# One transfer for V, a masked four-pass softmax and 128-column products in a decode step

## The chip, the cores and the metric

The kernel runs on one core of one Trainium2 chip. The metric is the device time of one execution in microseconds (us). Beside the unprofiled times there is one profiled execution; its span runs from the first to the last instruction, and the time of the execution is a little longer than its span. Engines are named as the profile names them: PE is TensorE's matrix multiplication and PEld its loading of weights, DVE is VectorE, ACT is ScalarE, POOL is GpSimd, SP is SyncE, which issues nearly all transfers of this kernel.

## The reference

One token of 1024 numbers passes two branches side by side, and their sum with the input is the result. All inputs and the output are bf16. `_layernorm` subtracts the mean and divides by the standard deviation.

```python
xn = layernorm(x)                                # [1, 1, 1024]
# branch A: 32 query heads over 4 key/value heads, the last W = 4096 of 65536 cached positions
q = (xn @ wq).reshape(32 heads, 128)             # wq [1024, 4096]
k = k_cache[:, :, Sk - W:, :]                    # [4 heads, 4096, 128], each for 8 query heads
v = v_cache[:, :, Sk - W:, :]
p = softmax(q @ k.T * 128 ** -0.5)
a = (p @ v).reshape(4096) @ wo                   # wo [4096, 1024]
# branch B
y = layernorm(xn)
b = gelu(y @ w1 + b1) @ w2 + b2                  # w1 [1024, 3584], w2 [3584, 1024]
out = x + a + b
```

With one token every weight is used once. wq and wo are 8 MB each, w1 and w2 7 MB each, the parts of K and V that are read 4 MB each: the 39.86 MB that the profile has as read from HBM.

## The kernel before

**What lies where.** `BIG` has 60 pieces of 1024 columns on each of 128 partitions. At first, pieces 0 to 31 hold wq (`WA`) and pieces 32 to 59 hold w1 (`W1`). Later W2 (28 pieces) lies in wq's place, and wo, 32 pieces, behind it. `KV` holds K as loaded, and later V; `KT` holds the turned K, and its end is used for the turned probabilities `PT`.

**The order of the transfers.** SP's queue is an order written out by hand: wq in two parts, K in two parts (two heads each), w1, then V in two parts, W2 in two parts (16 and 12 pieces) and wo in four (16, 11, 4 and 1 pieces). The first five are issued at once. A V part (L312) waits until VectorE has turned the K part in whose place it goes. W2 (issued by the helper `load_chunks`, L159; wo has L319) waits until the eight groups of q matmuls are done (`done["q"]`), since it overwrites wq. wo waits until the seven groups of the hidden layer are done (`done["h"]`), since it overwrites w1. ACT issues three small transfers (x, b1, b2).

**The order on TensorE.** A product that spreads x over the partitions; 38 matmuls on zeros as a warm-up, which begin when POOL has prepared all constants (`C["consts"]`); 64 matmuls for q, as soon as wq has landed; 32 for the scores, each half of K as soon as VectorE has turned it (L284); 56 for the hidden layer (`done["h"]`); a small product that adds up the sums of the exponentials and puts the sum where it is needed (`done["tot"]`, L484); four small ones that turn the hidden layer (`done["hT"]`); 32 for P times V (L496, `done["pv"]`); then eleven rounds of eight matmuls: seven for W2 and four for the first 16 pieces of wo. A round starts when `s_feed` has reached its count; POOL adds to that semaphore as W2's parts land and when the attention's result is ready (L407 to L414), and wo's first transfer adds to it too. The last 16 pieces of wo are multiplied in small matmuls of 32 columns as their transfers land, ending in L510.

**Softmax and P times V.** The scores lie in four banks of PSUM (`S`), 2048 columns on 128 partitions. VectorE finds the maximum of each row (L333), joins the partitions' maxima (L337, L339) and writes the bias `NMB` (L342). ScalarE then takes the exponential of all 2048 columns in one instruction with the sum of each row (L345), and VectorE turns the result in blocks of 32 (L349). A matmul of P times V takes 128 columns of weights from `PT`, in steps of 64, so that two neighbours overlap by half, and 2 x 256 columns of V:

```python
C["exp"] = ACT.mark(act.activation(
    out=Pb[:, :], in_=S, func=ACTF.Exp, bias=NMB[:, 0:1], scale=SCALE, accum_out=SUMP[:, 0:1]))
last = add(bank(1), PT[:, bass.ds(i * 256 + u * 64, 128)], V3[:, :, bass.ds(i * 1024 + u * 256, 256)])
```

VectorE reads rows 0 to 63 of the product and takes the right columns of each query head by the mask `HALF` while it divides by the sum (L380), adds them up (L385), turns the result (L388, L391), and ScalarE writes it as weights for wo (L394, L395).

Of the kernel before, what the change touches and what calls it, by code (L numbers as in the profile page):

```python
# [5 lines left out]
ALU = mybir.AluOpType  # L6
ACTF = mybir.ActivationFunctionType
AX = mybir.AxisListType

D = 1024  # L10
# [3 lines left out]
DH = 128  # L14
REP = HQ // HKV
SK = 65536
W = 4096
FC = F // 128
# [4 lines left out]
W2_CHUNKS = [16, 12]  # L23
# [4 lines left out]
PAIRS = 2  # L28
FAR = -1e30
XP = 72  # L30
TAIL = 16
# [4 lines left out]
ROUND = 4  # L36
# [17 lines left out]
def bass_parallel_sum__sliding_block_cached__mixer_channel_mlp__decode_kernel(  # L54
# [13 lines left out]
    SCALE = float(DH) ** -0.5  # L68
# [13 lines left out]
    s_w2 = sems("s_w2", len(W2_CHUNKS))  # L82

    DVE = Track(nc, "S_DVE")
    ACT = Track(nc, "S_ACT")
    POOL = Track(nc, "S_POOL")
    done = {n: nc.alloc_semaphore(f"S_PE_{n}") for n in (
        "x", "h", "hT", "q", "sc", "pv", "tot", "fin")}
    s_feed = nc.alloc_semaphore("S_FEED")

    def sb(name, shape, d):
        return nc.alloc_sbuf_tensor(name, shape, d)

    f32, bf16 = dt.float32, dt.bfloat16
    identb = sb("identb", [128, 128], bf16)
    identf = sb("identf", [128, 128], f32)
    onesb = sb("onesb", [2, 128], bf16)
    FLIP = sb("FLIP", [8, 8], bf16)
    E4 = sb("E4", [32, 4 * 128], bf16)
    B64 = sb("B64", [128, 64], f32)  # L100
    HALF4 = sb("HALF4", [64, 4], f32)
    HALF = sb("HALF", [64, PAIRS], f32)
    OTHER = sb("OTHER", [2, 128], bf16)
    ALT = sb("ALT", [2, 512], bf16)
    EDGE = sb("EDGE", [2, 132], bf16)
# [13 lines left out]
    MX2 = sb("MX2", [128, 2], f32)  # L119
    MX8 = sb("MX8", [32, 8], f32)  # L120
    MXR = sb("MXR", [32, 1], f32)
    NMB = sb("NMB", [128, 1], f32)
    Pb = sb("Pb", [128, 2048], bf16)
    XN = Pb[:, 0:1024]
    XM = Pb[:, 1024:2048]
    Q32 = Pb[:, 0:512]
    QTB = Pb[:, 512:1024]
    SUMP = sb("SUMP", [128, 1], f32)
    REC = sb("REC", [64, 1], f32)
    ON = sb("ON", [32, DH], f32)  # L130
    ONT = sb("ONT", [32, DH], f32)
    O2 = sb("O2", [128, 32], f32)
# [2 lines left out]
    ONM = QBD[0:32, :].bitcast(f32)  # L135
    KV = sb("KV", [128, 16384], bf16)
    KT = sb("KT", [128, 16384], bf16)
    PT = KT[:, 16384 - 2112:16384]
    BIG = sb("BIG", [128, KC * NQ + KC * F], bf16)
    WA, W1 = BIG[:, 0:KC * NQ], BIG[:, KC * NQ:KC * NQ + KC * F]  # L140
    W2 = WA[:, 0:FC * D]
    PS = nc.alloc_psum_tensor("PS", [128, 8 * 512], f32)
    PSb = PS[:, :].bitcast(bf16)

    def bank(n, rows=128, first=0):
        return PS[first:first + rows, n * 512:(n + 1) * 512]
# [23 lines left out]
    def pool_wait():  # L170
        pool.wait_ge(POOL.sem, POOL.cnt)
# [11 lines left out]
    POOL.mark(pool.memset(identf[:, :], 0.0))  # L183
    POOL.mark(pool.memset(FLIP[:, :], 0.0))
    POOL.mark(pool.memset(EDGE[:, :], 0.0))
    POOL.mark(pool.memset(HALF4[:, :], 1.0))
    POOL.mark(pool.memset(OTHER[:, :], FAR))
    POOL.mark(pool.memset(ALT[:, :], 0.0))
    POOL.mark(pool.memset(E4[:, :], 0.0))
# [15 lines left out]
    POOL.mark(pool.affine_select(  # L205
        out=ALT[:, :].rearrange("p (x g) -> p x g", g=2), in_=ALT[:, :].rearrange("p (x g) -> p x g", g=2),
        pattern=[[0, 256], [-1, 2]], compare_op=ALU.not_equal, fill=1.0, base=0, channel_multiplier=1))
    POOL.mark(pool.affine_select(
        out=HALF4[:, :], in_=HALF4[:, :], pattern=[[-16, 4]], compare_op=ALU.is_ge, fill=0.0,
        base=0, channel_multiplier=1))  # L210
    pool_wait()
    POOL.mark(pool.affine_select(
        out=HALF4[:, :], in_=HALF4[:, :], pattern=[[16, 4]], compare_op=ALU.is_ge, fill=0.0,
        base=15, channel_multiplier=-1))
    POOL.mark(pool.memset(GO[:, :], 0.0))
    pool_wait()
    POOL.mark(pool.tensor_tensor(out=HALF[:, :], in0=HALF4[:, 0:2], in1=HALF4[:, 2:4], op=ALU.add))  # L217
    C["consts"] = POOL.cnt

    act.wait_ge(POOL.sem, C["QBD"])  # L220
# [5 lines left out]
    def pairs(cache, c):  # L226
        return cache[0, 2 * c:2 * c + 2, SK - W:SK, :].rearrange("g (m i) d -> m g (i d)", m=64)
# [9 lines left out]
    def dve_wait():  # L237
        dve.wait_ge(DVE.sem, DVE.cnt)

    def layernorm_stats(src, n, name):  # L240
# [34 lines left out]
        XZ[:, :].rearrange("p (r w) -> p r w", r=KC)[:, :, 7:104:32], XNT[:, :].unsqueeze(2).to_broadcast([128, KC, 4])))  # L275
    dve.wait_ge(POOL.sem, C["consts"])
    DVE.mark(dve.tensor_reduce(
        out=B64[:, :].rearrange("p (k r) -> p k r", k=2),
        in_=identf[:, :].rearrange("p (q r) -> p r q", q=4).unsqueeze(1).to_broadcast([128, 2, 32, 4]),
        axis=AX.X, op=ALU.add))  # L280

    def turn_k(n):
# [23 lines left out]
    for n in range(2, 4):  # L306
        turn_k(n)

    V = KV[:, :]
    for c in range(PAIRS):  # L310
        sp.wait_ge(DVE.sem, C["kt", 2 * c + 1])
        sp.dma_start(V[:, c * 8192:(c + 1) * 8192], pairs(A_v_cache, c)).then_inc(s_v, 16)  # L312
    sp.wait_ge(done["q"], 8)
    load_chunks(W2, w2_p, W2_CHUNKS, D, s_w2)
    sp.wait_ge(done["h"], 7)
    c0 = 0
    for j, n in enumerate(WO_CHUNKS):
        first = (FC + c0) * D
        sp.dma_start(BIG[:, first:first + n * D], wo_flat[:, c0 * D:(c0 + n) * D]).then_inc(s_wo[j] if j else s_feed, HALF_FEED)  # L319
        c0 += n  # L320

# [16 lines left out]
    dve_wait()  # L338
    DVE.mark(dve.tensor_reduce(out=MXR[:, :], in_=MX8[:, :], axis=AX.X, op=ALU.max))  # L339
    dve_wait()  # L340
    for b in range(4):
        C["nmb"] = DVE.mark(dve.tensor_scalar(  # L342
            out=NMB[32 * b:32 * b + 32, :], in0=MXR[:, :], scalar1=-SCALE, scalar2=None, op0=ALU.mult))
    act.wait_ge(DVE.sem, C["nmb"])
    C["exp"] = ACT.mark(act.activation(  # L345
        out=Pb[:, :], in_=S, func=ACTF.Exp, bias=NMB[:, 0:1], scale=SCALE, accum_out=SUMP[:, 0:1]))

    dve.wait_ge(ACT.sem, C["exp"])
    C["d_pt"] = DVE.mark(dve.transpose(PT[:, 0:2048], Pb[:, :]))  # L349
    act.wait_ge(done["h"], 7)  # L350
    C["a_h8"] = ACT.mark(act.activation(out=H8, in_=bank(0, 8), func=ACTF.Copy))

# [19 lines left out]
        out=spread(0, FC // ROUND), in0=rows_of(HT[:, :]), in1=rows_of(U2[:, :]), op=ALU.mult))  # L372

    dve.wait_ge(done["tot"], 1)
    DVE.mark(dve.reciprocal(out=REC[:, :], in_=PS[0:64, 3 * 512:3 * 512 + 1]))
    dve_wait()
    dve.wait_ge(done["pv"], 8)
    for i in range(2):
        rows = slice(32 * i, 32 * i + 32)
        DVE.mark(dve.scalar_tensor_tensor(  # L380
            out=ONM.rearrange("p (i c d) -> p i c d", i=2, c=PAIRS)[:, i],
            in0=PS[rows, 512:1024].rearrange("p (c i d) -> p i c d", c=PAIRS, i=2)[:, i], scalar=REC[rows, 0:1],
            in1=HALF[rows, :].unsqueeze(2).to_broadcast([32, PAIRS, DH]), op0=ALU.mult, op1=ALU.mult))
    dve_wait()
    DVE.mark(dve.tensor_reduce(  # L385
        out=ON[:, :], in_=ONM.rearrange("p (g d) -> p d g", g=4), axis=AX.X, op=ALU.add))
    dve_wait()
    DVE.mark(dve.transpose(ONT[:, :], ON[:, :]))  # L388
    dve_wait()
# [33 lines left out]
    def add(to, lhsT, rhs, **place):  # L423
        return pe.matmul(to, lhsT=lhsT, rhs=rhs, start=False, stop=False, skip_group_check=True, **place)  # L424
# [56 lines left out]
        last.then_inc(done["h"], 1)  # L481

    pe.wait_ge(ACT.sem, C["exp"])
    pe.matmul(PS[0:64, 3 * 512:3 * 512 + 1], lhsT=B64[:, :], rhs=SUMP[:, :]).then_inc(done["tot"], 1)  # L484
    pe.wait_ge(ACT.sem, C["a_h8"])
    for c in range(4):
        last = add(turned[:, c], H8[:, c:512:4], FLIP[:, 0:7])
        if c == 0:
            pe.wait_ge(s_v, 32)
    last.then_inc(done["hT"], 1)  # L490

    pe.wait_ge(DVE.sem, C["d_pt"])
    V3 = V.rearrange("p (c x) -> p c x", c=PAIRS)
    with pe.Fori(0, 8) as i:
        for u in range(4):
            last = add(bank(1), PT[:, bass.ds(i * 256 + u * 64, 128)], V3[:, :, bass.ds(i * 1024 + u * 256, 256)])  # L496
        last.then_inc(done["pv"], 1)

    pe.wait_ge(DVE.sem, C["d_GT"])
    with pe.Fori(0, ROUNDS) as t:  # L500
        pe.wait_ge(s_feed, turn)
        pe.reg_add(turn, turn, 2 * HALF_FEED)
        for u in range(ROUND):
            for a in range(2):
                add(bank(7), GO[:, bass.ds(t * STEP + (LEAD + 2 * u - ROW - a), 128)],
                    BIG[:, bass.ds(t * (ROUND * D) + (u * D + a * 512), 512)])

    c0 = TAIL
    def add_held(to, lhsT, rhs, column):
# [5 lines left out]
    for j, n in enumerate(WO_ROWS[WO_HEAD:]):  # L515
        held = c0 + n == 32
        if held:
            for a in range(4):
                first = LEAD + 2 * (c0 - TAIL) - (0 if a % 2 else ROW)
                pe.ldweights(OT[:, first:first + 32], tile_position=(0, 32 * a))  # L520
        pe.wait_ge(s_wo[WO_HEAD + j], 16)
        for c in range(c0, c0 + n):
            rhs = BIG[:, (FC + c) * D:(FC + c + 1) * D]
            for a in range(4):
                first, column = LEAD + 2 * (c - TAIL) - (0 if a % 2 else ROW), 7 * 512 + a // 2 * 256
                to, of = PS[32 * a:32 * a + 32, column:column + 256], rhs[:, TAIL_AT[a]:TAIL_AT[a] + 256]
                if held:
                    last = add_held(to, OT[:, first:first + 32], of, 32 * a)
                else:
                    last = add(to, OT[:, first:first + 32], of, tile_position=(0, 32 * a))  # L530
        c0 += n
# [31 lines left out]
```

## Time and profile before

| | |
|---|---|
| median of 3 runs | 98.81 us (98.64 to 98.84) |
| time of the profiled execution | 98.62 us |
| its span | 97.2 us |
| granted TensorE clock | 1.00 |
| PE busy | 79.4 us (82%) |
| DVE busy | 39.0 us (40%) |
| ACT busy | 11.2 us (12%) |
| read from HBM | 39.86 MB, 410 GB/s over the span |

The profile's page divides the span into 40 equal slices and gives each engine's busy share in tenths; the row DMA gives the mean busy share of the core's 16 DMA engines. Its chain that ended last is followed back from the last instruction, each step to what released it. A group of instructions is given with its line, engine, operation, out<-in tiles, count, busy time, mean, and the idle time before it with what ended that. DMA issues are given with their size and the time from issue to landing; since all of SP's transfers pass one queue, that time holds the wait behind earlier transfers too. Matmuls that come from a helper all have its line (L424), so they are told apart by their tiles: `BIG,XZ` is q, `KT,QBD` the scores, `BIG,YZ` the hidden layer, `KV,KT` P times V, `BIG,GO` W2 and wo.

### The profile page before, as it was taken

How to read it: one execution, taken by the hardware profiler on the slowest of the kernel's cores; microseconds unless marked ns; L12 is line 12 of the kernel's file. 1: busy time of each engine (PE TensorE's matmuls, PEld its weight loads, DVE VectorE, ACT ScalarE, POOL GpSimd, SP SyncE). 2: the span in 40 equal slices, each digit the busy share in tenths (PEclk: the TensorE clock that was granted, in tenths of full speed). 3: DMA queues.
4: the chain of work that ended last, by engine and by line, in shares of the span. 5: the costliest groups of instructions: out<-in, count | busy, mean ns of one | idle time of the engine just before them, and what ended most of it. 6: DMA issues, size and time to landing. Idle time of an engine off the chain costs nothing.

```text
span 97.2 us, 1412 instructions
## 1 busy us (share of the span) xinstructions
PE 79.4 (82%) x389; PEld 33.4 (34%) x400; DVE 39.0 (40%) x54; ACT 11.2 (12%) x20; POOL 9.9 (10%) x27
## 2 busy tenths in 40 slices
PE   0000899977999999999299999899999999979982
PEld 0000134423444432343134444333334344334451
DVE  0000589840079986999945450060029000000001
ACT  0870000060000006000003500200000100000001
POOL 6999400000000000000000000000000000000000
DMA  2998888899999988889999999999899999899990
GB/s 64 651 473 378 378 378 378 378 458 432 401 431 549 590 378 378 378 378 401 415 431 431 431 492 431 431 458 394 384 475 499 458 431 431 368 389 436 388 379 3
DMA packets 1989, 39.88 MB, mean 410 GB/s; under 512 B 322, under 2 KB 324, under 8 KB 452
## 3 DMA queue, kind: packets, MB, share of 16 engines
q1 hardware_dynamic: 1876, 39.85, 95.7%
q10 hardware_dynamic: 112, 0.01, 0.1%
q8 instruction: 1, 0.02, 0.1%
HBM read 39.86 MB, written 0.00 MB: 410 GB/s over the span
## 4 chain that ended last, share of the span: by engine, by line
DMA 54%; PE 30%; DVE 11%; issue 1%; SPq 1%; ACT 1%
DMA BIG<-in_A_wo_dram 32%; PE PS L424 30%; DMA BIG<-in_A_wq_dram 22%; DVE KT L284 9%; SPq L319 1%; DVE Pb L292 1%; DVE QBD L303 1%; ACT Pb L290 1%; DVE Pb L401 0%; SPq L159 0%; PE PS L510 0%
## 5 line engine op out<-in xcount | busy, mean ns | idle before, releaser
L424 PE MATMUL PS<-BIG,GO 128*128 (+1 forms) x137 | 21.5, 334 | 1.8 <-POOLq L414 0.8
L284 DVE STREAM_TRANSPOSE KT<-KV 128x4096 bf16<-128x4096 bf16 x4 | 17.5, 4424 | 6.9 <-DMA KV<-in_A_k_cache_dram 6.9
L424 PE MATMUL PS<-BIG,XZ 128*128 x64 | 14.0, 379 | 1.3 <-DMA BIG<-in_A_wq_dram 1.3
L424 PEld LDWEIGHTS PS<-BIG,GO 128*128 (+1 forms) x148 | 9.9, 97 | 13.5 <-issue 5.9
L424 PE MATMUL PS<-BIG,YZ 128*128 x56 | 12.4, 380 | 0.1
L428 PE MATMUL PS<-QBD 128*128 128x512 bf16 x38 | 10.1, 434 | 0.4 <-POOL HALF L217 0.4
L424 PEld LDWEIGHTS PS<-BIG,XZ 128*128 x64 | 6.2, 97 | 9.0 <-issue 2.7
L424 PE MATMUL PS<-KT,QBD 128*128 x32 | 7.4, 380 | 1.9 <-DVE KT L284 1.9
L420 PE MATMUL PS<-XBRP,onesb 1*128 1x512 bf16 x2 | 1.0, 617 | 9.7 <-DMA XBRP<-in_A_x_dram 9.7
L424 PE MATMUL PS<-KV,KT 128*128 x32 | 8.3, 381 | 0.5
L401 DVE CAST Pb<-PS 64x256 bf16<-64x256 f32 x1 | 0.4, 416 | 20.0 <-PE PS L510 20.0
L424 PEld LDWEIGHTS PS<-BIG,YZ 128*128 x56 | 5.4, 96 | 7.1 <-issue 1.2
L428 PEld LDWEIGHTS PS<-QBD 128*128 128x128 bf16 x38 | 4.0, 108 | 6.9 <-issue 3.7
L242 DVE BATCH_NORM_STATS2 BN<-PS 128x6 f32<-128x512 f32 x2 | 1.3, 688 | 10.7 <-PE PS L420 10.7
L424 PEld LDWEIGHTS PS<-KT,QBD 128*128 x32 | 3.0, 97 | 6.2 <-issue 3.3
L424 PEld LDWEIGHTS PS<-KV,KT 128*128 x32 | 3.1, 96 | 5.3 <-issue 3.8
L380 DVE SCALAR_TENSOR_TENSOR QBD<-PS,REC,HALF 32x256 f32<-32x256 f32 x2 | 0.9, 474 | 6.8 <-PE PS L424 6.8
L345 ACT ACTIVATE Pb<-PS,NMB 128x2048 bf16<-128x2048 f32 x1 | 2.0, 1967 | 13.8 <-DVE NMB L342 13.8
L420 PEld LDWEIGHTS PS<-XBRP,onesb 1*128 1x128 bf16 x2 | 0.1, 108 | 9.7 <-DMA XBRP<-in_A_x_dram 9.7
L349 DVE STREAM_TRANSPOSE KT<-Pb 128x2048 bf16<-128x2048 bf16 x1 | 2.3, 2310 | 2.1 <-ACT Pb L345 2.1
L333 DVE TENSOR_REDUCE MX<-PS 128x1 f32<-128x1024 f32 x2 | 2.4, 1206 | 1.3 <-PE PS L424 1.3
L354 DVE COPY HT<-PS 128x28 f32<-128x28 f32 x1 | 0.2, 207 | 6.2 <-PE PS L424 6.2
(81 smaller groups left out, 42.1 us busy)
## 6 DMA issues: line engine op xcount, KB each, us to landing
BIG<-in_A_wq_dram SPq DMA_DIRECT2D x1, 7168.0 KB, 21.1
BIG<-in_B_w_dram SPq DMA_DIRECT2D x1, 7168.0 KB, 46.0
KV<-in_A_k_cache_dram SPq DMA_DIRECT2D x2, 2048.0 KB, 27.7
KV<-in_A_v_cache_dram SPq DMA_DIRECT2D x2, 2048.0 KB, 14.5
BIG<-in_B_w_dram SPq DMA_DIRECT2D x1, 4096.0 KB, 20.5
BIG<-in_A_wo_dram SPq DMA_DIRECT2D x1, 4096.0 KB, 23.1
BIG<-in_B_w_dram SPq DMA_DIRECT2D x1, 3072.0 KB, 27.1
BIG<-in_A_wo_dram SPq DMA_DIRECT2D x1, 2816.0 KB, 29.4
```

Of the source, the lines that this page charges most:

```text
L242: DVE.mark(dve.bn_stats(out=BN[:, 12 * n + 6 * i:12 * n + 6 * i + 6], in_=src[:, 512 * i:512 * i + 512]))
L284: C["kt", n] = DVE.mark(dve.transpose(KT[:, n * 4096:(n + 1) * 4096], KV[:, n * 4096:(n + 1) * 4096]))
L290: C["q32"] = ACT.mark(act.activation(out=Q32, in_=bank(7), func=ACTF.Copy))
L292: C["qtb"] = DVE.mark(dve.transpose(QTB, Q32))
L303: C["d_QBD"] = DVE.mark(dve.tensor_copy(to, of))
L319: sp.dma_start(BIG[:, first:first + n * D], wo_flat[:, c0 * D:(c0 + n) * D]).then_inc(s_wo[j] if j else s_feed, HALF_FEED)
L333: C["mx"] = DVE.mark(dve.tensor_reduce(out=MX2[:, n:n + 1], in_=S[:, 1024 * n:1024 * n + 1024], axis=AX.X, op=ALU.max))
L345: C["exp"] = ACT.mark(act.activation(out=Pb[:, :], in_=S, func=ACTF.Exp, bias=NMB[:, 0:1], scale=SCALE, accum_out=SUMP[:, 0:1]))
L349: C["d_pt"] = DVE.mark(dve.transpose(PT[:, 0:2048], Pb[:, :]))
L420: last = pe.matmul(bank(2 + i), lhsT=onesb[0:1, :], rhs=XB[0:1, 8 * i:8 * i + 8, :])
L424: return pe.matmul(to, lhsT=lhsT, rhs=rhs, start=False, stop=False, skip_group_check=True, **place)
L428: pe.matmul(to, lhsT=zeros[:, 0:128], rhs=zeros[:, 0:512], skip_group_check=True, **how)
```

## The change

V no longer goes into K's place in two transfers of two heads, but into the first 16 pieces of `BIG` (wq's place) in one transfer of four heads; each partition takes 128 positions of one head, 32 KB. It is issued after the q matmuls. W2 follows V in `BIG`, at pieces 16 to 43; its first part still goes into wq's place and is issued after q, its second part now overlaps w1's place and waits for the hidden layer. wo's first transfer goes to pieces 44 to 59, and the other three go where V was, so SP waits for P times V before it issues them.

The exponential is taken in four passes: for each half of the score columns, one pass for each pair of key/value heads, which reads and writes runs of two neighbouring columns in every four. Each pair has a bias of its own, with a very low number at the query heads of the other pair, so that the exponential is zero there. The result `P` has 4096 columns, with zeros, and is turned in two halves. A matmul of P times V then takes 128 columns of its own from `PT` and 512 columns of V in one run. The sums of the exponentials have four columns, which VectorE adds; the mask `HALF` goes, and four scalings of 128 columns take the place of two with a mask.

```diff
-    B64 = sb("B64", [128, 64], f32)
-    HALF4 = sb("HALF4", [64, 4], f32)
-    HALF = sb("HALF", [64, PAIRS], f32)
+    B128 = sb("B128", [128, 128], f32)
+    MASKC = sb("MASKC", [32, PAIRS], f32)
...
-    PT = KT[:, 16384 - 2112:16384]
+    P, PT = KT[:, 0:4096], KT[:, 4096:8192]
...
-    W2 = WA[:, 0:FC * D]
+    V, W2 = BIG[:, 0:TAIL * D], BIG[:, TAIL * D:(TAIL + FC) * D]
...
-    POOL.mark(pool.affine_select(
-        out=HALF4[:, :], in_=HALF4[:, :], pattern=[[-16, 4]], compare_op=ALU.is_ge, fill=0.0,
-        base=0, channel_multiplier=1))
-    pool_wait()
-    POOL.mark(pool.affine_select(
-        out=HALF4[:, :], in_=HALF4[:, :], pattern=[[16, 4]], compare_op=ALU.is_ge, fill=0.0,
-        base=15, channel_multiplier=-1))
+    for c in range(PAIRS):
+        POOL.mark(pool.affine_select(
+            out=MASKC[:, c:c + 1], in_=MASKC[:, c:c + 1], pattern=[[0, 1]], compare_op=ALU.is_ge, fill=FAR,
+            base=-16 if c else 15, channel_multiplier=1 if c else -1))
     POOL.mark(pool.memset(GO[:, :], 0.0))
-    pool_wait()
-    POOL.mark(pool.tensor_tensor(out=HALF[:, :], in0=HALF4[:, 0:2], in1=HALF4[:, 2:4], op=ALU.add))
...
-    V = KV[:, :]
-    for c in range(PAIRS):
-        sp.wait_ge(DVE.sem, C["kt", 2 * c + 1])
-        sp.dma_start(V[:, c * 8192:(c + 1) * 8192], pairs(A_v_cache, c)).then_inc(s_v, 16)
     sp.wait_ge(done["q"], 8)
-    load_chunks(W2, w2_p, W2_CHUNKS, D, s_w2)
+    sp.dma_start(V, A_v_cache[0, :, SK - W:SK, :].rearrange("g (m i) d -> m g (i d)", m=32)).then_inc(s_v, 16)
+    load_chunks(W2, w2_p, W2_CHUNKS[:1], D, s_w2)
     sp.wait_ge(done["h"], 7)
+    load_chunks(W2, w2_p, W2_CHUNKS[1:], D, s_w2[1:], W2_CHUNKS[0])
     c0 = 0
     for j, n in enumerate(WO_CHUNKS):
-        first = (FC + c0) * D
+        first = (c0 - TAIL if j else TAIL + FC) * D
+        if j == 1:
+            sp.wait_ge(done["pv"], 8)
...
+    DVE.mark(dve.tensor_scalar(out=MXN[:, :], in0=MXR[:, :], scalar1=-SCALE, scalar2=None, op0=ALU.mult))
+    dve_wait()
     for b in range(4):
         C["nmb"] = DVE.mark(dve.tensor_scalar(
-            out=NMB[32 * b:32 * b + 32, :], in0=MXR[:, :], scalar1=-SCALE, scalar2=None, op0=ALU.mult))
+            out=NMB[32 * b:32 * b + 32, :], in0=MASKC[:, :], scalar1=MXN[:, 0:1], scalar2=None, op0=ALU.add))
     act.wait_ge(DVE.sem, C["nmb"])
-    C["exp"] = ACT.mark(act.activation(
-        out=Pb[:, :], in_=S, func=ACTF.Exp, bias=NMB[:, 0:1], scale=SCALE, accum_out=SUMP[:, 0:1]))
-
-    dve.wait_ge(ACT.sem, C["exp"])
-    C["d_pt"] = DVE.mark(dve.transpose(PT[:, 0:2048], Pb[:, :]))
+    half = 2048
+    for r in range(2):
+        for c in range(PAIRS):
+            C["exp"] = ACT.mark(act.activation(
+                out=P[:, r * half:(r + 1) * half].rearrange("p (i m g) -> p i m g", i=64, m=8)[:, :, :, 2 * c:2 * c + 2],
+                in_=S.rearrange("p (i m g) -> p i m g", i=64, m=8)[:, :, :, 2 * r:2 * r + 2],
+                func=ACTF.Exp, bias=NMB[:, c:c + 1], scale=SCALE, accum_out=SUMP[:, 2 * r + c:2 * r + c + 1]))
+        dve.wait_ge(ACT.sem, C["exp"])
+        C["d_pt"] = DVE.mark(dve.transpose(PT[:, r * half:(r + 1) * half], P[:, r * half:(r + 1) * half]))
...
     dve.wait_ge(done["tot"], 1)
-    DVE.mark(dve.reciprocal(out=REC[:, :], in_=PS[0:64, 3 * 512:3 * 512 + 1]))
+    DVE.mark(dve.tensor_reduce(
+        out=TOT[:, :], in_=PS[:, 3 * 512:3 * 512 + 2 * PAIRS], axis=AX.X, op=ALU.add))
+    dve_wait()
+    DVE.mark(dve.reciprocal(out=REC[:, :], in_=TOT[:, :]))
     dve_wait()
     dve.wait_ge(done["pv"], 8)
-    for i in range(2):
-        rows = slice(32 * i, 32 * i + 32)
-        DVE.mark(dve.scalar_tensor_tensor(
-            out=ONM.rearrange("p (i c d) -> p i c d", i=2, c=PAIRS)[:, i],
-            in0=PS[rows, 512:1024].rearrange("p (c i d) -> p i c d", c=PAIRS, i=2)[:, i], scalar=REC[rows, 0:1],
-            in1=HALF[rows, :].unsqueeze(2).to_broadcast([32, PAIRS, DH]), op0=ALU.mult, op1=ALU.mult))
+    for j in range(4):
+        DVE.mark(dve.tensor_scalar(
+            out=ONM[:, 128 * j:128 * j + 128], in0=PS[32 * j:32 * j + 32, 512 + 128 * j:512 + 128 * j + 128],
+            scalar1=REC[32 * j:32 * j + 32, 0:1], scalar2=None, op0=ALU.mult))
...
     with pe.Fori(0, 8) as i:
         for u in range(4):
-            last = add(bank(1), PT[:, bass.ds(i * 256 + u * 64, 128)], V3[:, :, bass.ds(i * 1024 + u * 256, 256)])
+            last = add(bank(1), PT[:, bass.ds(i * 512 + u * 128, 128)], V[:, bass.ds(i * 2048 + u * 512, 512)])
...
-                    BIG[:, bass.ds(t * (ROUND * D) + (u * D + a * 512), 512)])
+                    BIG[:, bass.ds(t * (ROUND * D) + ((TAIL + u) * D + a * 512), 512)])
...
-            rhs = BIG[:, (FC + c) * D:(FC + c + 1) * D]
+            rhs = BIG[:, (c - TAIL) * D:(c - TAIL + 1) * D]
```

More of the change, by code (lines that the diff above doesn't have):

```diff
@@ L121, in bass_parallel_sum__sliding_block_cached__mixer_channel_mlp__decode_kernel @@
     MXR = sb("MXR", [32, 1], f32)
-    NMB = sb("NMB", [128, 1], f32)
+    MXN = sb("MXN", [32, 1], f32)
+    NMB = sb("NMB", [128, PAIRS], f32)
     Pb = sb("Pb", [128, 2048], bf16)
@@ L127, in bass_parallel_sum__sliding_block_cached__mixer_channel_mlp__decode_kernel @@
     QTB = Pb[:, 512:1024]
-    SUMP = sb("SUMP", [128, 1], f32)
-    REC = sb("REC", [64, 1], f32)
+    SUMP = sb("SUMP", [128, 2 * PAIRS], f32)
+    TOT = sb("TOT", [128, 1], f32)
+    REC = sb("REC", [128, 1], f32)
     ON = sb("ON", [32, DH], f32)
@@ L185, in bass_parallel_sum__sliding_block_cached__mixer_channel_mlp__decode_kernel @@
     POOL.mark(pool.memset(EDGE[:, :], 0.0))
-    POOL.mark(pool.memset(HALF4[:, :], 1.0))
+    POOL.mark(pool.memset(MASKC[:, :], 0.0))
     POOL.mark(pool.memset(OTHER[:, :], FAR))
@@ L277, in bass_parallel_sum__sliding_block_cached__mixer_channel_mlp__decode_kernel @@
     DVE.mark(dve.tensor_reduce(
-        out=B64[:, :].rearrange("p (k r) -> p k r", k=2),
-        in_=identf[:, :].rearrange("p (q r) -> p r q", q=4).unsqueeze(1).to_broadcast([128, 2, 32, 4]),
+        out=B128[:, :].rearrange("p (k r) -> p k r", k=4),
+        in_=identf[:, :].rearrange("p (q r) -> p r q", q=4).unsqueeze(1).to_broadcast([128, 4, 32, 4]),
         axis=AX.X, op=ALU.add))
@@ L374, in bass_parallel_sum__sliding_block_cached__mixer_channel_mlp__decode_kernel @@
     dve.wait_ge(done["tot"], 1)
-    DVE.mark(dve.reciprocal(out=REC[:, :], in_=PS[0:64, 3 * 512:3 * 512 + 1]))
+    DVE.mark(dve.tensor_reduce(
+        out=TOT[:, :], in_=PS[:, 3 * 512:3 * 512 + 2 * PAIRS], axis=AX.X, op=ALU.add))
+    dve_wait()
+    DVE.mark(dve.reciprocal(out=REC[:, :], in_=TOT[:, :]))
     dve_wait()
     dve.wait_ge(done["pv"], 8)
-    for i in range(2):
-        rows = slice(32 * i, 32 * i + 32)
-        DVE.mark(dve.scalar_tensor_tensor(
-            out=ONM.rearrange("p (i c d) -> p i c d", i=2, c=PAIRS)[:, i],
-            in0=PS[rows, 512:1024].rearrange("p (c i d) -> p i c d", c=PAIRS, i=2)[:, i], scalar=REC[rows, 0:1],
-            in1=HALF[rows, :].unsqueeze(2).to_broadcast([32, PAIRS, DH]), op0=ALU.mult, op1=ALU.mult))
+    for j in range(4):
+        DVE.mark(dve.tensor_scalar(
+            out=ONM[:, 128 * j:128 * j + 128], in0=PS[32 * j:32 * j + 32, 512 + 128 * j:512 + 128 * j + 128],
+            scalar1=REC[32 * j:32 * j + 32, 0:1], scalar2=None, op0=ALU.mult))
     dve_wait()
     DVE.mark(dve.tensor_reduce(
-        out=ON[:, :], in_=ONM.rearrange("p (g d) -> p d g", g=4), axis=AX.X, op=ALU.add))
+        out=ON[:, :], in_=ONM.rearrange("p (j d) -> p d j", j=4), axis=AX.X, op=ALU.add))
     dve_wait()
@@ L483, in bass_parallel_sum__sliding_block_cached__mixer_channel_mlp__decode_kernel @@
     pe.wait_ge(ACT.sem, C["exp"])
-    pe.matmul(PS[0:64, 3 * 512:3 * 512 + 1], lhsT=B64[:, :], rhs=SUMP[:, :]).then_inc(done["tot"], 1)
+    pe.matmul(PS[:, 3 * 512:3 * 512 + 2 * PAIRS], lhsT=B128[:, :], rhs=SUMP[:, :]).then_inc(done["tot"], 1)
     pe.wait_ge(ACT.sem, C["a_h8"])
@@ L488, in bass_parallel_sum__sliding_block_cached__mixer_channel_mlp__decode_kernel @@
         if c == 0:
-            pe.wait_ge(s_v, 32)
+            pe.wait_ge(s_v, 16)
     last.then_inc(done["hT"], 1)
     pe.wait_ge(DVE.sem, C["d_pt"])
-    V3 = V.rearrange("p (c x) -> p c x", c=PAIRS)
     with pe.Fori(0, 8) as i:
         for u in range(4):
-            last = add(bank(1), PT[:, bass.ds(i * 256 + u * 64, 128)], V3[:, :, bass.ds(i * 1024 + u * 256, 256)])
+            last = add(bank(1), PT[:, bass.ds(i * 512 + u * 128, 128)], V[:, bass.ds(i * 2048 + u * 512, 512)])
         last.then_inc(done["pv"], 1)
```

## The prediction

> **What bounds the kernel now.** I read the page's head and busy rows first, then the chain of waits, then the DMA issues with their landings, then the PE rows of the last third. The page's head, the DMA row (busy tenths in 40 slices) and the queue rows say that the transfers hardly pause:
>
> ```profile
> span 97.2 us, 1412 instructions
> ...
> PE 79.4 (82%) x389; PEld 33.4 (34%) x400; DVE 39.0 (40%) x54; ACT 11.2 (12%) x20; POOL 9.9 (10%) x27
> ...
> DMA  2998888899999988889999999999899999899990
> ...
> q1 hardware_dynamic: 1876, 39.85, 95.7%
> ...
> q8 instruction: 1, 0.02, 0.1%
> ```
>
> SyncE's queue alone keeps 16 engines busy for 95.7% of the span; the rest is its two ends. The chain of waits ends in a transfer too (columns: start, length, what):
>
> ```profile
> 49.89 12.45 PE PS L424 x56
> 62.34 0.02 issue
> 62.35 0.33 SPq L319
> ...
> 63.20 31.34 DMA BIG<-in_A_wo_dram
> 94.53 0.04 issue
> 94.58 0.73 PE PS L424 x20
> ```
>
> Those 31.34 us look as if an earlier issue at 62.35 would help. The landings say no. A stretch of DMA issues at a time gives KB of each and us from issue to landing; here are the second V load (issued 47.4), both of W2 (48.0 and 48.6) and the large first one of wo (62.4):
>
> ```profile
> KV<-in_A_v_cache_dram SPq DMA_DIRECT2D x1, 2048.0 KB, 11.4
> BIG<-in_B_w_dram SPq DMA_DIRECT2D x1, 4096.0 KB, 20.5
> BIG<-in_B_w_dram SPq DMA_DIRECT2D x1, 3072.0 KB, 27.1
> BIG<-in_A_wo_dram SPq DMA_DIRECT2D x1, 4096.0 KB, 23.1
> ```
>
> Issue plus time to landing gives the clock of the queue: W1 lands at 49.0 (3.0 + 46.0), the first V at 53.9 (36.2 + 17.7), the second at 58.8, W2 at 68.5 and 75.7, wo at 85.5, 92.2 (62.8 + 29.4), 94.5 and 95.2. The gaps are 4.9, 4.9, 9.7, 7.2, 9.8, 6.7, 2.3, 0.7 us for 2048, 2048, 4096, 3072, 4096, 2816, 1024 and 256 KB: 418 to 427 KB a us for every large one. So each transfer follows on the one before without a hole, whenever it was issued, and the end is the last landing plus 0.3 us of matmuls and 1.7 us of eviction and store. TensorE runs just behind; its rows of the last stages (start, busy, what, idle before it) show by how much:
>
> ```profile
> 63.32 8.73 PE L424 MATMUL PS<-KV,KT 128*128 x32
> 72.14 12.79 PE L424 MATMUL PS<-BIG,GO 128*128 x49
> 85.69 8.55 PE L424 MATMUL PS<-BIG,GO 128*128 x68 [0.77 <-POOLq L414]
> 94.58 0.73 PE L424 MATMUL PS<-BIG,GO 128*32 128x256 bf16 x20 [0.33 <-DMA BIG<-in_A_wo_dram]
> ```
>
> It has 0.77 us to spare before wo's first 4096 KB and 0.33 more before the last rows: 1.1 us of delay in P times V reaches nothing.
>
> **The change part by part.**
>
> *Transfers.* The bytes are the same, one issue of about 0.54 us goes, and V's rows are 32 KB in place of 16 KB. By the gaps, V took 9.8 us for 4096 KB, W2's rows of 32 KB 9.7, wo's rows of 32 KB 9.8: a saving of 0 to 0.1 us. I take 0.05.
>
> *When V is issued.* Before: at 36.2 and 47.4, behind the key transposes. After: once, after the eighth q matmul group (36.4), W2's first part right behind it. W1 holds the queue until 49.0, so nothing starts earlier or later: 0.
>
> *SyncE's order.* W2's second part is moved behind the wait for the hidden layer (62.35), since it now overwrites W1. The queue needs it when W2's first part is through, at 68.5. The final store goes from issue (96.03) to the end of the span in 1.2 us, so by 63.6 packets can flow: 4.9 us of cover. wo's first load is issued one issue later (0.43 us), at 62.8, for a need at 75.7. The last three wo loads now wait for P times V, as they overwrite V: 72.1 against a need at 85.5, 13 us of cover, and only they and the final store stand behind that wait. If the hidden layer came x us beyond 67.3, or P times V beyond 84.3, the end would move by x. Both cost 0.
>
> *Softmax.* The bias takes one more VectorE instruction, 0.15 us by its 32x1 neighbours plus a 0.05 wait, so exp starts at 52.93 in place of 52.73. Four passes of 1024 elements replace one of 2048. ScalarE's copy of 128x1024 takes 1.03 us, and the reading of the accumulator 0.19: at least 4 x 1.22 = 4.9, ending at 57.8. Dearest row for strided elements: 64 of them take 0.298 us (L305) where one takes 0.202 (L249), 1.5 ns each, so 0.2 + 1.54 + 0.19 = 1.93 a pass, 7.7 us, ending at 60.6. I take 4.9: L345, the same operation on the same tile, runs at 0.96 ns an element. The second transpose (2.31) then ends at 60.2, at worst 63.0. Before it, P times V cannot start: TensorE is on the hidden layer until 62.25 and on its turning until 63.29. So +2.8 to +5.5 us on ScalarE cost 0; cover gone, every us beyond 63.3 eats the 1.1 first. ScalarE's next task waits for the hidden layer at 62.35 anyway.
>
> *P times V.* 32 matmuls with 128 columns of weights and 512 of data before and after; only the steps differ. I keep 8.73 us. From below q's 64 take 13.99, 0.219 each, 7.0 in all; from above the warm-up's 434 ns each, 13.9. A gain is worth nothing (W2's rounds are held up by the wait at 85.69); the upper end would cost 5.2 - 1.1 = 4.1 us, and no row of a large loop after 15 us comes near it.
>
> *After it.* A sum over four columns joins the reciprocal before P times V ends: hidden. Four scalings of 32x128 replace two of 32x256 at 0.474: between 4 x 0.15 and 4 x 0.474, against 0.95, so -0.4 to +0.9 us on a chain that ends at 75.9 and is needed with wo at 85.5. 0.
>
> *W2's rounds.* Their address gains a constant, perhaps one register instruction in about 70 of a round of 1.8 us: 0.03 x 7 = 0.2 us before the 0.77, 0.1 in the four wo rounds before the 0.33. 0.
>
> *Set-up.* GpSimd loses a 0.19 us addition and two waits, so the warm-up (11.12) starts up to 0.44 earlier and ends earlier, but wq lands at 22.33 all the same. The ones-pattern on VectorE doubles (0.60 to about 1.2) inside 6.9 idle us. 0.
>
> Sum: 98.62 for the profiled execution, less 0.05, is 98.57. It lies 0.19 below the median of 98.81, so on medians 98.75. A measurement of this kernel can tell about 0.2% from no change (the three runs span 0.20 us).
>
> [...] Row: wo's transfers read 32 KB or less every 64 KB, and run at 418 to 420 KB a us; W2's rows, 56 KB apart, at 422 to 427. [...] V's four heads now lie far apart in one transfer with 32 KB steps inside. [...]
>
> **The rivals.**
>
> *Slower, V's stream.* Four heads side by side read less well. For it: the four-head order is new. Against: two heads, wo and W2 all run within 2%. The slowest large stretch is wq, 8192 KB from about 1.8 to 22.33, 400 KB a us with its start-up, 5% below 422: V then takes 0.5 us more, all on the end since the queue has no slack: 99.3. It decides from a V landing gap of 10.0.
>
> *Slower, late P times V.* Passes above (60.9 + 1.1 - 52.93) / 4 = 2.27 us each, or a like slowdown of the matmuls. For it: more strided work on ScalarE than any row has. Against: both bounds stay under. At 2.5 us a pass: +0.9 us, 99.7.
>
> *Slower, the instruction packet.* One 16 KB instruction packet runs beside the data; the trace has it between 94.6 and 94.7, when nearly all data is through. An address change in TensorE's loops shifts the code behind it. Were it to come before an engine's last rows, that engine finishes one 16 KB packet later, about 0.6 us (4.9 us for 8 packets an engine): 99.4. Against: a shift by an instruction or two moves it hardly. [...]
>
> *Faster.* Each transfer's start has a cost that the gaps hide, and V is now one. Largest that rows leave: K's two took 9.7 us from 22.33 to 32.05, V's 9.8, so a few tenths at most: 0.3, 98.5.
>
> *A hole in the queue*, if the packets of a late issue need longer than the 6.15 us from 62.35 to 68.5; at 7.3 us, +1.1: 99.9. Against: the store's 1.2 us.
>
> **How the numbers follow.** Forecast (queue full, 98.75, own range 98.55 to 98.95) 0.58; within it 0.50 counts as no change, 0.06 faster, 0.02 slower. V's stream 0.10, late P times V 0.07, instruction packet 0.07, hole 0.03: slower in all 0.29. Faster start 0.15: faster in all 0.21. Same 0.50. The range leaves out the late and the holed case and the edges of the others: 98.4 to 99.4.
>
> **What would show it.** Right: V lands 9.7 to 9.8 us after W1 (near 58.7), W2 at 68.4 and 75.6, wo at 85.4 to 95.1; four exp passes of 1.0 to 1.2 us ending by 58 to 61; P times V starting at 63.3; idle time of about 0.8 before wo's rounds. Wrong: a V gap over 10, a DMA slice below 8 tenths between 63 and 70, P times V starting after 64.4, or no idle time left before wo's rounds.

## The result and the profile after

The changed kernel takes 99.59 us (median of six runs, 99.45 to 99.84) against 98.70 for the kernel before on the same chip: a ratio of 1.0084 (95% interval 1.0066 to 1.0103), 0.84% slower. The profiled execution took 99.82 us with a span of 98.6 us, 1.35 us longer than before. That lies outside the predicted range of 98.4 to 99.4. Two executions of later runs (109.66 us in e15, 107.61 us in e18), at granted clocks of 0.953 and 0.968, are left out of every ratio.

The page's head, the DMA row and the queue rows of the changed kernel:

```profile
span 98.6 us, 1434 instructions
...
DMA  2998888959999888899499999999999999999850
...
q1 hardware_dynamic: 1732, 39.85, 94.5%
...
q8 instruction: 1, 0.02, 0.1%
q14 instruction: 1, 0.01, 0.0%
```

The queue still has no hole between its ends, and it moves the same 39.85 MB. (The DMA row counts a packet whole in the slice in which it starts; by the packet records of the trace the 16 engines are 99 to 100% busy in every 2 us from 4 to 94, the slices with a 5 and a 4 too.) New is the last row: one packet of 0.01 MB of instructions on a queue of its own, q14, beside the 16 KB packet on q8 that was there before. The DMA issues, KB and us from issue to landing, of V (issued 36.6), W2's two parts (37.2, 62.4) and wo's first two (62.8, 72.2):

```profile
BIG<-in_A_v_cache_dram SPq DMA_DIRECT2D x1, 4096.0 KB, 22.4
BIG<-in_B_w_dram SPq DMA_DIRECT2D x1, 4096.0 KB, 31.5
BIG<-in_A_wo_dram SPq DMA_DIRECT2D x1, 4096.0 KB, 23.8
BIG<-in_B_w_dram SPq DMA_DIRECT2D x1, 3072.0 KB, 13.5
BIG<-in_A_wo_dram SPq DMA_DIRECT2D x1, 2816.0 KB, 21.2
```

With W1 landing at 49.2 (3.0 + 46.2), the queue's clock now reads 59.0, 68.7, 75.9, 86.6 and 93.4, so gaps of 9.8, 9.7, 7.2, 10.7 and 6.8 us. All are those of before within 0.1 us but one: wo's first 4096 KB took 10.7 in place of 9.8. Most of the 1.35 us is lost there, between 75.9 and 86.6 (0.2 were lost before W1's landing, and 0.2 come behind the last data packet: from its end to the end of the span it is 2.52 us, before 2.34). It is lost by a single DMA engine: by the packet records, 15 engines are through with that transfer by 85.18, the last at 86.18.

TensorE's rows (start, busy, what, idle before it) say that it was not late:

```profile
63.40 8.73 PE L427 MATMUL PS<-BIG,KT 128*128 x32
72.22 12.85 PE L427 MATMUL PS<-BIG,GO 128*128 x56
86.92 8.58 PE L427 MATMUL PS<-BIG,GO 128*128 x72 [1.85 <-POOLq L417]
95.91 0.73 PE L427 MATMUL PS<-BIG,GO 128*32 128x256 bf16 x20 [0.41 <-DMA BIG<-in_A_wo_dram]
```

P times V starts at 63.40 (before 63.32) and takes the same 8.73 us; the idle time ahead of wo's rounds has grown from 0.77 to 1.85. And in the 0.2 us around 76.7, when VectorE has just run its last piece of the attention's end (76.1), the queues show what met wo's data:

```profile
q1 hardware_dynamic: 4, 0.13, 152.7%
...
q14 instruction: 1, 0.01, 10.2%
```

In the packet records, that 8 KB packet runs from 76.71 for 0.325 us, and the 32 KB packet behind it on the same engine takes 1.875 us where the median is 1.216: 0.98 us lost by one engine. The transfer has landed only at 86.6, behind that engine's last packet.

### The profile page after: what moved, and what is told of

Read it like the earlier page. It is cut to its first block, busy times and chain, and to the rows that moved or that the text cites. A ratio compares the mean times of both kernels' runs of the same rounds, so it can differ in the third digit from the quotient of the medians.

```text
span 98.6 us, 1434 instructions
## 1 busy us (share of the span) xinstructions
PE 81.0 (82%) x400; PEld 33.8 (34%) x400; DVE 42.7 (43%) x59; ACT 13.6 (14%) x26; POOL 9.6 (10%) x26
## 3 DMA queue, kind: packets, MB, share of 16 engines
q1 hardware_dynamic: 1732, 39.85, 94.5%
## 4 chain that ended last, share of the span: by engine, by line
DMA 45%; PE 38%; DVE 11%; issue 2%; ACT 1%; SPq 1%
PE PS L427 38%; DMA BIG<-in_A_wo_dram 24%; DMA BIG<-in_A_wq_dram 21%; DVE KT L280 9%; DVE Pb L288 1%; DVE QBD L299 1%; ACT Pb L286 1%; ACT H L353 1%; DVE Pb L404 0%; SPq L160 0%; SPq L315 0%; PE PS L512 0%
## 5 line engine op out<-in xcount | busy, mean ns | idle before, releaser
L427 PE MATMUL PS<-BIG,GO 128*128 (+1 forms) x148 | 22.2, 337 | 2.4 <-POOLq L417 1.9
L431 PE MATMUL PS<-QBD 128*128 128x512 bf16 x38 | 11.1, 465 | 0.0
L427 PE MATMUL PS<-BIG,KT 128*128 x32 | 8.3, 381 | 0.5
L346 ACT ACTIVATE KT<-PS,NMB 128x1024 bf16<-128x1024 f32 x4 | 4.4, 1112 | 14.3 <-DVE NMB L340 14.3
L351 DVE STREAM_TRANSPOSE KT<-KT 128x2048 bf16<-128x2048 bf16 x2 | 4.5, 2291 | 2.4 <-ACT KT L346 2.4
L427 PEld LDWEIGHTS PS<-BIG,KT 128*128 x32 | 3.1, 96 | 5.3 <-issue 3.8
L384 DVE TENSOR_SCALAR QBD<-PS,REC 32x128 f32<-32x128 f32 x4 | 1.4, 345 | 6.7 <-PE PS L427 6.6
## 6 DMA issues: line engine op xcount, KB each, us to landing
BIG<-in_B_w_dram SPq DMA_DIRECT2D x1, 7168.0 KB, 46.2
```

The costliest lines, as they stand in the source:

```text
L346: C["exp"] = ACT.mark(act.activation(out=P[:, r * half:(r + 1) * half].rearrange("p (i m g) -> p i m g", i=64, m=8)[:, :, :, 2 * c:2 * c + 2],
L351: C["d_pt"] = DVE.mark(dve.transpose(PT[:, r * half:(r + 1) * half], P[:, r * half:(r + 1) * half]))
L384: DVE.mark(dve.tensor_scalar(out=ONM[:, 128 * j:128 * j + 128], in0=PS[32 * j:32 * j + 32, 512 + 128 * j:512 + 128 * j + 128], scalar1=REC ...
L431: pe.matmul(to, lhsT=zeros[:, 0:128], rhs=zeros[:, 0:512], skip_group_check=True, **how)
```

## The experiments

Two theories stood at first. **Instruction theory**: VectorE's program has grown from 101 to 109 instructions (waits counted), so VectorE fetches 8 KB more of them, amid the data. **Transfer theory**: the new place, form or order of V, W2 and wo costs the time. A third, the **place theory**, came from the first eight runs. Ratios are to the kernel before on the same chip, with 95% intervals.

| run | edit | ratio | 8 KB packet on q14 |
|---|---|---|---|
| e1 | before, +8 VectorE | 1.0089 (1.0072 to 1.0105) | at 76.7 |
| e2 | before, +8 ScalarE | 1.0044 (1.0028 to 1.0061) | none |
| e3 | after, -9 VectorE | 1.0038 (1.0024 to 1.0052) | none |
| e4 | after, V in two | 1.0099 (1.0083 to 1.0116) | at 76.7 |
| e5 | before, unchanged | 1.0001 (0.9987 to 1.0015) | none |
| e6 | before, +4 VectorE | 1.0031 (1.0021 to 1.0042) | at 97.8 |
| e7 | before, +2 ScalarE | 1.0035 (1.0025 to 1.0046) | none |
| e8 | before, +6 GpSimd | 1.0040 (1.0025 to 1.0055) | none |
| e9 | before, 32 bytes of padding | 1.0057 (1.0040 to 1.0074) | none |
| e10 | before, +8 VectorE, tiles in place | 1.0059 (1.0043 to 1.0076) | at 76.6 |
| e11 | after, tiles in place | 1.0048 (1.0031 to 1.0065) | at 78.8 |
| e12 | after, -9 VectorE, tiles in place | 0.9991 (0.9981 to 1.0001) | none |
| e13 | before, 128 bytes of padding | 1.0023 (1.0009 to 1.0036) | none |
| e14 | before, +4 VectorE, tiles in place | 0.9988 (0.9975 to 1.0001) | at 97.4 |
| e15 | e12 with V in two | 1.0010 (0.9992 to 1.0027) | none |
| e16 | e12 at multiples of 512 bytes | 0.9976 (0.9962 to 0.9989) | none |
| e17 | before at multiples of 512 bytes | 1.0004 (0.9995 to 1.0013) | none |
| e18 | e12 once more | 0.9990 (0.9975 to 1.0005) | none |

**The instructions alone, and two counter-tests (e1 to e4).** The dummy copies read a constant and write a small tile that nobody reads, declared ahead of `NMB` (in this and the other excerpts "..." marks lines left out):

```diff
+    SCR = sb("SCR", [32, 16], f32)
     NMB = sb("NMB", [128, 1], f32)
...
+    for i in range(8):
+        DVE.mark(dve.tensor_copy(SCR[:, 2 * i:2 * i + 2], identf[0:32, 0:2]))
```

> The kernel before with eight more VectorE copies of 32x2 numbers behind the ones-pattern, in idle time (VectorE then has 109 instructions in its program, as the changed kernel has, in place of 101); nothing reads what they write. Instruction theory (VectorE's longer program makes it fetch one more 8 KB packet of instructions while data flows, and the DMA engine that carries it ends 1 us late): about 99.5 us, +0.8 to +0.9%, a q14 instruction packet on the page, and wo's first transfer landing 10.7 us after W2's last in place of 9.8. Transfer theory (the new place and order of V, W2 and wo cost the time): 98.7, no q14 packet, gap 9.8.

e2 has a wait and seven such copies on ScalarE in their place.

> The kernel before with eight more instructions for ScalarE (a wait and seven copies of 32x2 numbers, in idle time before q), nothing for VectorE. Instruction theory in its form for VectorE alone: 98.7 us, no q14 packet, since ScalarE's program is short (47 instructions). If it is the whole program's length that counts: about 99.5 and a q14 packet. Transfer theory: 98.7.

e3 is the changed kernel with a shorter VectorE program:

```diff
...
-    DVE.mark(dve.tensor_scalar(out=MXN[:, :], in0=MXR[:, :], scalar1=-SCALE, scalar2=None, op0=ALU.mult))
-    dve_wait()
+    pool.wait_ge(DVE.sem, C["mxr"])
+    POOL.mark(pool.tensor_scalar(out=MXN[:, :], in0=MXR[:, :], scalar1=-SCALE, scalar2=None, op0=ALU.mult))
+    pool_wait()
     for b in range(4):
-        C["nmb"] = DVE.mark(dve.tensor_scalar(
+        C["nmb"] = POOL.mark(pool.tensor_scalar(
...
-        dve.wait_ge(ACT.sem, C["exp"])
-        C["d_pt"] = DVE.mark(dve.transpose(PT[:, r * half:(r + 1) * half], P[:, r * half:(r + 1) * half]))
+    dve.wait_ge(ACT.sem, C["exp"])
+    C["d_pt"] = DVE.mark(dve.transpose(PT, P))
```

> The changed kernel with nine VectorE instructions fewer (100): the bias is made by GpSimd, and the probabilities are turned in one instruction of 4096 columns behind the fourth pass. All transfers as in the changed kernel. Instruction theory: no q14 packet, wo's first transfer lands 9.8 us after W2's last, 98.6 to 98.7 us, so the same as before or up to 0.1% faster. Transfer theory: 99.5, as the changed kernel. The single turn ends near 62.5, before P times V can start, under both.

e4 is the changed kernel with V as two transfers of 16 KB a partition:

```diff
-    sp.dma_start(V, A_v_cache[0, :, SK - W:SK, :].rearrange("g (m i) d -> m g (i d)", m=32)).then_inc(s_v, 16)
+    for i in range(2):
+        sp.dma_start(V[:, i * 8192:(i + 1) * 8192], A_v_cache[0, :, SK - W:SK, :].rearrange(
+            "g (m i) d -> m g (i d)", m=32)[:, :, i * 8192:(i + 1) * 8192]).then_inc(s_v, 16)
...
-            pe.wait_ge(s_v, 16)
+            pe.wait_ge(s_v, 32)
```

> The changed kernel with V in two transfers of 16 KB a partition, to the same place and at the same point of the queue. Instruction theory: as the changed kernel, 99.5 to 99.7 us with its q14 packet; the 16 KB rows cost 0 to 0.1 us. Theory that the 32 KB rows or the single transfer cost the time: 98.7.

e1 gave the whole loss to the kernel before, whose transfers nobody had touched: +0.89%, with the new packet on its page and wo's first transfer 24.0 us in landing where it had taken 23.1.

```profile
q14 instruction: 1, 0.01, 0.0%
```

```profile
BIG<-in_A_wo_dram SPq DMA_DIRECT2D x1, 4096.0 KB, 24.0
```

So the order, place and form of the transfers aren't needed for the loss, and e4 agrees: V in two is no better. But the instruction theory missed twice. e2 and e3 have no q14 packet and still lose 0.4%, where about nothing was expected. Half of the loss was still unexplained, and e1 held some of it.

**Which edits bring the other half (e5 to e8).**

> The kernel before, unchanged, as a kernel of its own, to see what two builds of the same differ by, and for a trace beside those of the runs so far. If the rest of 0.4% that the kernels without a q14 packet showed is an accident of a build or of its place in memory, it can show here too: 98.7 to 99.2. If it comes from the edits: 98.75, with the first part of wq landing about 4.2 us after its issue, as in the profile before.

> The kernel before with four more VectorE copies of 32x2 numbers (105 instructions in its program). Instruction theory: either a q14 packet and 99.5 to 99.7 us, then the limit lies at 102 to 105, or no q14 packet and 98.7 to 99.2, then it lies at 106 to 109. Nothing in between with a q14 packet in the data.

> The kernel before with one wait and one copy of 32x2 numbers more on ScalarE, in idle time. If a longer ScalarE program as such costs the 0.4% that eight more showed, by its length: 98.8 to 98.9. If any edit of the program can bring it (another place of the code, a later start of one DMA engine): 98.7 or 99.2, by chance. Instruction theory for VectorE: no q14 packet.

> The kernel before with six more short memory fills on GpSimd behind its constants (nobody waits for them in time). If only VectorE's and ScalarE's programs matter: 98.75. If any engine's longer program delays the start of the first transfer: 99.1 to 99.3, with the first part of wq landing 4.5 us after its issue or later. No q14 packet by either.

A second build of the same kernel is the same (1.0001), so building again does not bring the loss. Four VectorE, two ScalarE or six GpSimd instructions all cost 0.3 to 0.4%, and eight on ScalarE (e2) cost about as much as two (e7). What these kernels have in common, and share with the changed kernel, is a small tile that is new or of another size ahead of the large ones. Tiles lie one behind another as they are declared. In the kernel before, `KV`, `KT` and `BIG` begin at bytes 37632, 70400 and 103168 of a partition, all odd multiples of 256. The changed kernel has `B128` in place of `B64` (256 bytes more) and other small tiles, and its `BIG` begins at 103456, 32 bytes past a multiple of 256. `SCR` had moved it by 32 or 64.

**Each cause alone, and both away (e9 to e12).** The padding is one line ahead of `KV`, `[128, 8]` in e9 and `[128, 56]` in e11 and e12; in e10 `SCR` is declared behind `BIG` instead:

```diff
+    PAD = sb("PAD", [128, 56], f32)
     KV = sb("KV", [128, 16384], bf16)
```

> The kernel before with 32 unused bytes a partition ahead of the tile that holds K, so that K's, the turned K's and the weights' tiles begin 32 bytes later; no instruction more. In the kernel before these tiles begin at a multiple of 256 bytes (37632, 70400, 103168); in the changed kernel and in all of the runs so far that were slower by 0.3 to 0.4% or more they don't, since the new or larger small tiles ahead of them move them. Place theory (transfers to a place that is no multiple of 256 bytes are slower): 99.15 us, +0.35%, packets of 24 KB 0.916 us in place of 0.912. Theory that more instructions of any engine cost 0.35%: 98.8.

> The kernel before with eight more VectorE copies of 32x2 numbers as in the first run, but with the tile that they write behind all others, so that nothing else moves. Instruction theory: q14 packet, one DMA engine 1 us late. Together with the place theory, 0.35% of the first run's 0.89% go: 99.2 to 99.5 us. Place theory alone: 98.75. Theory that the q14 packet explains it all: 99.65.

> The changed kernel with 224 unused bytes a partition ahead of K's tile, so that it and the tiles behind it begin at multiples of 256 bytes; 109 VectorE instructions as in the changed kernel. Both theories together: q14 packet, 99.2 to 99.5 us (the place's share gone, the packet's left). Place theory alone: 98.7. q14 packet alone: 99.6.

> The changed kernel with both taken away: nine VectorE instructions fewer (bias by GpSimd, one turn of 4096 columns) and the same 224 bytes. Both theories together: no q14 packet, 98.65 to 98.75 us, as before or 0.1% faster by V's 32 KB rows. If the new transfers or their order cost anything by themselves: above 98.85.

e9 adds no instruction at all and loses 0.57% by 32 bytes. That is more than the 0.35% expected, and more than e6 lost by the same 32 bytes (0.31%); why the size differs is not shown. e10 and e11 have the instructions alone and lose 0.59% and 0.48%. For the changed kernel the parts add up: 0.38% for the place alone (e3) and 0.48% for the instructions alone (e11) make 0.86%, and it lost 0.84%. e12 is the changed kernel with all its transfers, its four passes and its 128-column products, without the two costs: 0.9991. Its issue of wo's first transfer (at 63.0) and its last TensorE rows stand within 0.2 us of those of before:

```profile
BIG<-in_A_wo_dram SPq DMA_DIRECT2D x1, 4096.0 KB, 22.6
```

```profile
85.85 8.58 PE L428 MATMUL PS<-BIG,GO 128*128 x68 [0.60 <-POOLq L418]
94.72 0.73 PE L428 MATMUL PS<-BIG,GO 128*32 128x256 bf16 x20 [0.29 <-DMA BIG<-in_A_wo_dram]
```

**How each cause works (e13 to e18).** e13 and e17 are e9 with 128 and 256 bytes; e14 is e10 with four copies; e15 joins e4's and e12's edits; e16 is e12 with 480 bytes of padding.

> The kernel before with 128 unused bytes a partition ahead of K's tile: the large tiles begin at an odd multiple of 128 bytes. Shifts of 32 and 64 bytes have cost 0.3 to 0.6%. If multiples of 128 are enough: 98.8. If 256 is needed: 99.1 to 99.3, 24 KB packets of 0.915 to 0.917 us.

> The kernel before with four more VectorE copies of 32x2 numbers (105 instructions), the tile that they write behind all others. The sixth run had its q14 packet only at 97.8 us, when the data was through. Both theories together: a q14 packet behind the data on the page, and 98.8 us, as before: a packet of instructions costs only where it meets data. If the packet costs by itself, or four instructions do: 99.1 or more.

> The changed kernel with both causes taken away, as in the twelfth run, and V in two transfers of 16 KB rows in place of one of 32 KB rows. What the rows are worth by themselves: by packet times (256 x 0.612 against 128 x 1.213 us over 16 engines) 0.09 us; by the landings before 0.04. So 98.75 to 98.85 where the twelfth run had 98.72; above 98.95 the rows matter more than thought.

> The twelfth run's kernel with the large tiles at multiples of 512 bytes in place of 256. If 256 is all that counts: 98.7, the same as before or 0.1% faster. If larger multiples go on helping: 98.5 or less, and faster than both kernels.

> The kernel before with 256 unused bytes a partition ahead of K's tile: the large tiles begin at multiples of 512 bytes in place of odd multiples of 256. If the sixteenth run's 0.24% come from the 512: 98.55 to 98.65 here too. If they come from the change itself (V's rows, shorter waits): 98.8, the same as before.

> The twelfth run's kernel once more, beside the one above on the same chip, for a narrower interval: it gave 0.9991 (0.9981 to 1.0001). If the change without its two causes is worth the 0.05 us that was predicted: ratio 0.999 to 1.000; if the sixteenth run's gain is the change's own and not that of 512 bytes: 0.997 to 0.998.

e14 settles the refill. Its page has the same packet as e1's and e10's, but its queue rows from 0 to 95.2 us don't: it comes at 97.4, when the data is through, and the kernel is as fast as before.

```profile
q1 hardware_dynamic: 1872, 39.85, 97.8%
q10 hardware_dynamic: 112, 0.01, 0.1%
q8 instruction: 1, 0.02, 0.1%
```

So in these kernels the packet cost only where it met data: a ratio of 0.9988 in e14, of 1.0059 in e10, where it comes at 76.6. With 101 instructions or fewer VectorE asked for none within the span, with 105 only behind its last piece of work (ended at 96.2 in e14), with 109 behind its last piece of the attention's end. That it is VectorE's is shown by these counts, since eight more on ScalarE and six more on GpSimd brought none, and by its time: it comes 0.5 to 0.9 us behind that piece in all five kernels, also in e11, whose piece ended late, at 77.9 in place of 75.8 to 76.3.

The place shows at two points. In the stream, the median packet of 24 KB takes 0.912 us in every run whose tiles begin at a multiple of 256 or 512 bytes, 0.913 off by 128 (e13, where 0.915 to 0.917 was expected), 0.914 off by 64 (e1, e2, e7, e8) and 0.915 off by 32 (the changed kernel, e3, e4, e6, e9); wo's packets of 32 KB go from 1.213 to 1.215 or 1.216. Added up for one engine, the data packets take 93.03 to 93.23 us in the ten kernels off a multiple of 256, and 92.73 to 93.07 in the ten on one. And at the end: from the end of the last data packet to the end of the span it is 2.49 to 2.66 us in the ten kernels off, and 2.34 to 2.42 in eight of those on. The other two, e16 and e18, have 2.65 and 2.83; their profiled executions had a granted clock of 0.983 (as had e11's, with 2.41), so their tails are not compared. The last rows on TensorE of e9, and then of e17, show the same (start, busy, idle before):

```profile
95.22 0.73 PE L425 MATMUL PS<-BIG,GO 128*32 128x256 bf16 x20 [0.45 <-DMA BIG<-in_A_wo_dram]
95.89 0.27 PE L511 MATMUL PS<-BIG,GO 128*32 128x256 bf16 x4
```

```profile
94.83 0.73 PE L425 MATMUL PS<-BIG,GO 128*32 128x256 bf16 x20 [0.33 <-DMA BIG<-in_A_wo_dram]
95.45 0.27 PE L511 MATMUL PS<-BIG,GO 128*32 128x256 bf16 x4
```

The last four matmuls follow the twenty by 0.62 us in e17 and by 0.67 in e9, and the twenty start 0.36 and 0.52 us after their data's last packet. Why a packet to such a place takes longer is not shown by these runs. The place alone does not account for it, for not every packet to a moved tile is longer: in all twenty kernels the packets of wq (56 KB, median 2.116 us) and of K (16 KB, 0.611) take the same, though their tiles are moved as well. The few ns appear only behind about 30 us: the 56 KB packets of W1, which start there, take 2.119 us in the mean in the changed kernel and 2.117 in the kernel before, those of wq 2.124 in both. So 32 bytes are shown to be enough for the loss, but not how they act.

For the kernel before, 512 bytes are no better than 256 (e17). e16 is the fastest kernel of all, 0.24% under the kernel before, between its two expectations; e18, the same at 256, is 0.1% under with an interval that touches 1. Where e16's last 0.1% come from is left open. With V's rows of 16 KB in place of 32 KB, e15 lies 0.2% above e12 and e18, within the intervals, so no gain by the longer rows is shown.

## Why the prediction was wrong

*What bounds the kernel.* Right: the queue stayed full, and the time is the last landing plus a tail. The tail was taken as constant, but grew by 0.18 us. The same fact made the outcome: with no slack, the loss of 0.98 us by one engine of sixteen took wo's first gap from 9.8 to 10.7 us and moved the kernel's end with it.

*Transfers, "a saving of 0 to 0.1 us".* **This step failed by a term that it lacked**: where in a partition the data is put. Bytes, rows and issues were counted, but not that the diff's first lines resize small tiles and so move `KV`, `KT` and `BIG` off a multiple of 256. Its price is 0.38% in the changed kernel (e3) and 0.23 to 0.57% in the kernel before (e9 and e13 with nothing else, e6 with four copies that cost nothing in e14; e2, e7 and e8 lie between). The saving itself, 0.05 us, fits e12 and e18 (0.999), but is too small for them to show.

*Softmax, "a cost of 0", and "After it", 0.* On the path, right. The groups of the changed kernel (busy, mean ns, idle before):

```profile
L346 ACT ACTIVATE KT<-PS,NMB 128x1024 bf16<-128x1024 f32 x4 | 4.4, 1112 | 14.3 <-DVE NMB L340 14.3
L340 DVE TENSOR_SCALAR NMB<-MASKC,MXN 32x2 f32<-32x2 f32 x4 | 0.9, 218 | 0.1
L384 DVE TENSOR_SCALAR QBD<-PS,REC 32x128 f32<-32x128 f32 x4 | 1.4, 345 | 6.7 <-PE PS L427 6.6
```

A pass takes 1.11 us (predicted 1.03 to 1.74 without the accumulator), and the last ends at 57.8 as predicted, but by two errors that cancel: the passes begin at 53.27, 0.34 us later than counted, mostly because the four bias instructions take 0.22 us each (0.14 before), and they follow each other every 1.10 us in place of 1.22, since the reading of the accumulator overlaps its pass by about 0.1. The second turn ends at 60.1. **But these steps counted an added instruction only by its time on its engine.** Eight more on VectorE also made its program longer, and that brought the fetch, where the prediction had put nothing: 0.59 and 0.48% alone (e10, e11).

*When V is issued, SyncE's order, P times V, W2's rounds, set-up.* All right: landing gaps of 9.8, 9.7 and 7.2 for V and W2, P times V starting at 63.40 and taking 8.73 us, 12.85 for W2's rounds (0.06 more, 0.2 allowed), warm-up from 10.71. None of the prediction's signs of being wrong came: V's gap, the DMA slices between 63 and 70 us and the start of P times V are as forecast, and the idle time before wo's rounds grew. What missed is a figure among its signs of being right, wo's first landing, at 86.6 us in place of 85.4.

*The rivals.* "The instruction packet" had the mechanism, one engine late by a packet, and a like size (99.4; e11 alone 99.22), but looked at the wrong one: it took the 16 KB packet at the end, moved by a shift in TensorE's code, and gave it 0.07. The packet was a second one, of 8 KB, brought by VectorE's count. It isn't free for the data: it cost 0.84 to 0.99 us of one DMA engine. V's stream (landing gap 9.8), late P times V and the hole in the queue didn't occur, and a faster start isn't shown (e12 and e18, 0.999). The range took one such mishap at a time; here an instruction packet and the place, of which no rival speaks, came together.

## What to carry to other kernels

Where a queue of transfers bounds the kernel without slack, look at what a change does to the engines' programs and to the addresses of the large tiles before its arithmetic: here a resized constant ahead of them cost 0.38% (e3) and the longer VectorE program 0.48% (e11), and the change with its three added passes of softmax cost nothing without the two (0.9991, e12). Try the large tiles at a multiple of 256 bytes (32 bytes off cost the kernel before 0.57% in e9, 128 off 0.23% in e13, and 512 gave it nothing more in e17, 1.0004), and compare instruction rows (q8, q14) on the page as well as data rows. When a kernel loses a little without a visible cause, add the suspected side effect alone to the kernel before: eight idle instructions and 32 bytes told more here than any part of the change.

## What was not expected of the hardware

The 8 KB instruction packet cost its DMA engine nearly three times its own time: 0.31 us for itself and 0.54 more on the data packet behind it (1.753 for 1.213 us, e10); 0.66 more (1.875 for 1.216 us in the changed kernel) where the data goes to a place off 256 bytes (the changed kernel, e1, e4). And the 16 KB packet on q8, beside the last data, takes 0.93 us in seven of the ten kernels with tiles at multiples of 256 bytes but 1.08 to 1.13 in all ten without; the other three (e16, e17, e18) have 0.99, 1.05 and 1.37, so the place is not all that sets it.
